# The opening of an attention stage: four first rotations on VectorE, the first row maxima in two parts, three loads of constants, and a new order of issue

## Chip, cores and metric

The kernel runs on one core of one Trainium2 chip. The metric is the device time of one execution in microseconds; the kernel before takes 635.73 us, the median of three runs between 634.97 and 636.86.

## What is computed

Three stages follow each other in one launch. Attention has 2 batches of 8 heads, 576 positions, 64 values per head, all in float32. A dense two-layer block (512 to 2048 to 512, leaky ReLU) takes its output, and a mixture of eight experts with the best two for each token takes that. The change touches attention alone:

```python
def rotate(x):
    x1, x2 = (x[..., :half], x[..., half:])
    return np.concatenate([x1 * cos - x2 * sin, x1 * sin + x2 * cos], axis=-1)
q_rot, k_rot = (rotate(q), rotate(k))
scores = scale * np.matmul(q_rot, k_rot.transpose(0, 1, 3, 2))
scores = scores - np.max(scores, axis=-1, keepdims=True)
attn = np.exp(scores)
attn = attn / (np.sum(attn, axis=-1, keepdims=True) + 1e-09)
return np.matmul(attn, v).astype(np.float32)
```

## The kernel before

Attention works through eight pairs of heads (pr = 0 to 7). The 576 positions of a head lie as five tiles j = 0 to 4 of 128 positions (the last one holds 64). A pair goes through these steps, each of which has a letter in the string ORDER (line 491):

- l (k for the first pair): the DMAs of q and k into raw; w: those of v. Part 0 of a load has the first 512 positions, part 1 the last 64. All go through SP's queue, apart from the first pair's second head and the constants, which go through ScalarE's queue.
- O on VectorE or P on GpSimd (POOL): the rotation ("rope"), four instructions: one product with cos (L299), two with sin, one for each half (L302), and one sum (L304). All of their inputs lie in SBUF. For the first pair each head is rotated for itself, so there are four ropes of four instructions on half-size tiles: q and k of head 0, q and k of head 1. FIRST_V (line 229) lists those on VectorE, FIRST_G those on POOL. All ropes of later pairs run on POOL.
- Q and K: TensorE transposes the rotated q and k into PSUM (L322, L324, L329). h and i: ScalarE copies them out as a rounded "high" part (L339). j and n: VectorE takes the rest as the "low" part (L343).
- M: for the row maxima, TensorE multiplies the high parts of q and k (L356), one tile of queries at a time. D: VectorE takes the maximum over the keys (L363 for the first pair, L368 later). J joins two halves of it (L374).
- R: TensorE turns the maxima into rows (L380); m: ScalarE copies those into MR (L384).
- S: the scores, keys on the partitions, as three products of high and low parts and one that takes MR off (L401). A cell is one tile j of keys by one half z (288) of the queries, both heads. W: ScalarE's exponential (L405).
- V: TensorE's product with v (L418). + on VectorE and ^ on POOL add exponentials (L425); G adds those up over the keys on TensorE (L434). U, t, T, s, B, N, X and Y divide by the sums and split the result into high and low for the dense block.
- The signs ! # $ % & * convert the dense block's first weights, o is a product on zeros that only keeps TensorE at work, c loads constants, f fills tiles on POOL, F and Z load weights and small inputs.

The order is written out by hand: every engine issues its instructions in the sequence in which their letters stand in ORDER, and each waits for its inputs and for the buffers it writes. The digit behind Q, K, M, R and S is one of three PSUM slots (two banks each) that the step writes; the step waits until the slot's last reader is done. A fourth pair of banks holds the products on zeros and later the output of V. The rotated tiles and their temporaries (rope_t) have two buffers each, which go round over (pair, q) and (pair, k). SP's queue follows ORDER as well.

After the last V of pair 7 TensorE goes on with the dense block (L570, L579), whose first part needs only the first batch's output.

Of the kernel before, what the change touches and what calls it, by code (L numbers as in the profile page):

```python
# [10 lines left out]
F32 = mybir.dt.float32  # L11
# [4 lines left out]
AF = mybir.ActivationFunctionType  # L16
# [5 lines left out]
B, H, S, D = 2, 8, 576, 64  # L22
# [3 lines left out]
KT = 5  # L26
# [10 lines left out]
_CUT = {}  # L37
# [44 lines left out]
def fused_kernel(ctx, tc, q, k, v, w_in, w_out, w_gate, w_noise, noise, w1, w2, consts, out):  # L82
    nc = tc.nc
    V, A, G, T = nc.vector, nc.scalar, nc.gpsimd, nc.tensor

    def pool(name, bufs=1, **kw):
        return tc.tile_pool(name=name, bufs=bufs, reuse_waits="tile", **kw)
# [23 lines left out]
    ident = const("ident")
# [109 lines left out]
    ct_att = ap.tile([128, NATT], F32, name="ct_att")  # L221
    a2 = att.enter_context(pool("att2", bufs=2))
    ps_s = att.enter_context(pool("ps_s", space=PSUM))
    ps_o = att.enter_context(pool("ps_o", space=PSUM))

    NP = B * 4
    NSET, NPB = 3, 10
    GROUPS, ADDERS = ((0, 1), (2, 3), (4,)), ((0,), (1,))
    FIRST_V, FIRST_G, ROPE_V = (('q', 0), ('k', 0), ('q', 1)), (('k', 1),), ()
    ET = mybir.EngineType  # L230
    order = ExitStack()
    order.enter_context(tc.manual_schedule(engines={ET.PE, ET.Activation, ET.DVE, ET.Pool}))
# [4 lines left out]
    raw, VF, VT, peak, MR = [], [], [], [], []  # L237
# [68 lines left out]
    def ps(n, name, shape=(128, 2, 512), dt=F32):  # L306
        return ps_s.tile(list(shape), dt, name=name, tag=f"s{n}")

    turned = {}

    def here(a):
        return slice(0, 128) if a is None else slice(64 * a, 64 * a + 64)

    def turn(pr, n, a, at):


        r = roped[pr, n][0]
# [12 lines left out]
        turned[pr, n, a] = p[:, :, :KT * 64].rearrange("p w (j n) -> p j w n", n=64)  # L330
# [39 lines left out]
    rows = {}  # L370
# [2 lines left out]
        with nc.allow_low_precision(reason="what is taken off is the same in a row's every place"):  # L373
            V.tensor_tensor(peak[pr % 2][:, :, 0:65:64].rearrange("p j h -> p h j"), halves[pr, 0], halves[pr, 1], op=OP.min)  # L374

    def max_turn(pr, at):
        p = ps(at, "pR")
        for j in range(KT):
            for w in range(2):
                T.matmul(p[:65, w, j * 64:(j + 1) * 64], peak[pr % 2][here(w), j], ident_r[here(w), here(w)], start=True, stop=True)  # L380
        rows[pr] = p[:65, :, :KT * 64].rearrange("p w (j n) -> p j w n", n=64)

    def max_rows(pr):
        A.activation(MR[pr % 2][:65].rearrange("p (j w n) -> p j w n", j=KT, w=2), rows[pr], AF.Copy)  # L384
# [104 lines left out]


    ORDER = (
"ckfcokkokkofokkokfoooooIOofoOoOoOoOQ0lOOoFohOoOZK1OlOooiOoloPM2wM0DPQ1lPDlM2hoPlDM0oPlDK2wjM0iwooPDlM1oPlDM0ol"
"DPM1oDM0oDPM1loDZQ0lnhPR1oomjoPoS2PS1WS0WS2PlWK1lWS0+liPVwVWnFPM2!S0DM1PWVDM2S0DM1PlWDS2lM0S1WDPWM2PQ0DM1hPDM2"
"VVDVj^lM1K2lDM0iVZ^DVlVJnwPM1R0wDS2mF+WS1PM0M2WDVP!GDPM1S0DGWPM2Q1DM0hGDS2PUjM0PWDtS1PM2WS0DlM1WS2wDPS0lW+S1ZW"
"K2PWS0Ti+M1sVPWwVDVwPVJnM0R1DBM2^mVDM0S1DPM2WVDM0S1DPM2WGDPM0S1DPS2W#Q0WS1hM2NVDWVjM2K1^DM0iVDVPGJnwM2S0lDPM1l"
"WGDlPM2US0DlS1PWl+M2VZWVwVDPlR0$lS1mM2lVPWtVDV^M0wS1DS2WP+S0WM1V^WVDM2S0DPS1WQ2WM0GPDhGTVjVPG%wM1PUK0sS2wDiPVt"
"VWnS1!PM2S0WBDVWJM1lS2DlR0W+Vlm^M1S2DS0W#S1NWM2V&DVW+PQ0M2S1hT^DsVWGwjlPM2S1DlM0PWGDFVM2S1PDS0WS2X+M1PVWGDWVYM"
"0wUS2DS1wJW+K0BWV*Vi^tVXnR2M1wPmVDV#M0M2S1DNVWDS0PXM1M2DGWVDPM1S0DS2W$Q1^WS0!M2VDhVPWVjYM2S0DS1W$S2PWM0GWPGDM1"
"US2DS0TWK1J%WVFVi^VwnR2wS0%msS1+WFM2VWD^V&M0S1DS2W+S0BWM1#V*WGwDV!tM2$S0M1WVDVGNDGVTsYM0US2DS1%&S0tWV+WVF+V&wV"
"#Xw*VwWS2$BS1WS0W^S2!M1VDWV^W%VM0M1M2VDN&GDGGYDXVJTR0#UsY$mtS1S2WBS0*WS1%WS2TWV+sV&*FVWZ+S0S1*WNS2BWS0WS1F^WGZ"  # L500
"VXV^WVVVNGGVYVXUYt")
    pairs = [(pr, n) for pr in range(NP) for n in "qk"]
    some = range(1, NP)
    both = [(0, n, a) for n in "qk" for a in range(2)]
    first = [(0, n, i, slice(a, a + 1), x) for a, x in enumerate((nc.sync, nc.scalar)) for n in "qk" for i in range(2)]
    spare = ps_o.tile([128, 2, 512], F32, name="pW", tag="o")
    cells = [(pr, j, z) for pr in range(NP) for j in range(KT) for z in range(2)]
    work = {"o": (lambda: busy(spare[:, 0]), [()] * ORDER.count("o")),
            "c": (lambda i: nc.scalar.dma_start(*((ct_att, consts[:, :NATT]), (ct, consts[:, NATT:NID]))[i]),
                  [(0,), (1,)]),  # L510
            "k": (load_qk, first),
            "l": (load_qk, [(pr, n, i, s) for pr, n in pairs[2:] for i, s in
                            [(0, slice(0, 2))] + ([(1, slice(0, 2))] if n == "q" else [(1, slice(a, a + 1)) for a in range(2)])]),
# [4 lines left out]
            "P": (rope, [(0, n, G, i, a, a + 1) for n, a in FIRST_G for i in range(4)] +  # L518
                  [(pr, n, G, i) for pr, n in pairs[2:] if (pr, n) not in ROPE_V for i in range(4)]),
            "Q": (turn, [(0, "q", 0), (0, "q", 1)] + [(pr, "q", None) for pr in some]),  # L520
            "K": (turn, [(0, "k", 0), (0, "k", 1)] + [(pr, "k", None) for pr in some]),
            "w": (load_v, [(pr, i) for pr in range(NP) for i in range(3)]),
            "M": (max_scores, [(0, a, j) for a in range(2) for j in range(KT)] +
                  [(pr, z, j) for pr in some for j in range(KT) for z in range(2)]),
            "S": (scores, cells), "W": (exp, cells), "V": (values, cells),
            "Z": (load_small, [(i,) for i in range(7)]), "F": (load_part, [(p,) for p in range(2 * NEARLY + 3)])}
# [543 lines left out]
    busy = nc.values_load(most, min_val=0, max_val=NT)  # L1070
    with tc.If(busy > C):
        with ExitStack() as rest:
# [13 lines left out]
            with tc.For_i(0, E, 1) as e:  # L1086
                n = nc.values_load(nparts[:, bass.ds(e, 1)], min_val=0, max_val=8)
                with tc.If(n > 0):
# [7 lines left out]
                    with tc.For_i(0, n, 1):  # L1096
# [4 lines left out]
                        t = bank[4][:CO, :5]  # L1101
# [49 lines left out]
```

## Time and profile before

| | us |
|---|---|
| runs: median, lowest, highest | 635.73, 634.97, 636.86 |
| the profiled execution's own time | 637.35 |
| its span, first to last instruction | 635.4 |
| TensorE's first score product (L401) | 19.66 |
| TensorE's first weights of the dense block (L570) | 149.03 |

TensorE counts as busy for 97% of the span, VectorE for 63%, ScalarE for 48%, POOL for 31%. In what follows PE is TensorE's products, PEld its weight loads, DVE is VectorE, ACT ScalarE, SP the queue that issues most DMAs. A row of the timeline gives the start and the duration in us, the engine, the line, what is written from what, how many instructions were merged into the row, and in brackets how long the engine was idle before it and what ended that. Products are pipelined, so the weight loads tell best when TensorE takes up a step.

### The profile page before, as it was taken

The page shows a single profiled execution, that of the slowest core. Times are in us where ns is not written, and L with a number is a line of the kernel's source. Part 1 is how long each engine was busy: PE and PEld are TensorE (multiplying, and loading weights), DVE is VectorE, ACT ScalarE, POOL GpSimd, SP SyncE. Part 2 cuts the span into 40 slices and gives each one's busy share as a digit, 9 for nine tenths or more (in the row PEclk, how much of TensorE's full clock was granted, in tenths as well). Part 3 has the DMA queues.
Part 4 walks back from the last instruction along what each step waited for, and adds up shares of the span by engine and source line. Part 5 has one row for each costly group of instructions (what it writes and reads, how often), then busy time and mean ns, then how long its engine had stood idle before and what let it go on. Part 6 is the DMA issues. An engine that isn't in the chain of part 4 may idle for free. (4 is left out here: it accounts for less than half of the span.)

```text
span 635.4 us, 12547 instructions
## 1 busy us (share of the span) xinstructions
PE 619.5 (97%) x4839; PEld 512.0 (81%) x4840; DVE 403.4 (63%) x844; ACT 303.3 (48%) x612; POOL 197.3 (31%) x203
## 2 busy tenths in 40 slices
PE   9999999999999999999999999999999999999993
PEld 4676676767888888897999768888888888888892
DVE  6788788784998888532476555647474747474511
ACT  2564565665554455222355414536453645454521
POOL 7999988354200000000000012140414141413202
PEclk9999999999999999999999999999999999999997
DMA  6332130333467544402744234485847585757413
GB/s 189 113 88 78 42 109 22 108 102 95 143 201 258 195 133 144 173 2 72 243 121 145 85 92 143 132 195 154 208 141 200 148 208 143 214 137 210 103 24 43
DMA packets 79167, 85.04 MB, mean 134 GB/s; under 512 B 11136, under 2 KB 60416, under 8 KB 79104
## 3 DMA queue, kind: packets, MB, share of 16 engines
q1 hardware_dynamic: 73760, 73.03, 38.1%
q0 software_dynamic: 4608, 10.49, 8.2%
q8 instruction: 39, 0.64, 0.4%
q10 hardware_dynamic: 736, 0.69, 0.4%
q14 instruction: 24, 0.20, 0.1%
HBM read 69.95 MB, written 14.19 MB: 132 GB/s over the span
## 5 line engine op out<-in xcount | busy, mean ns | idle before, releaser
L213 DVE TENSOR_TENSOR wl<-raw,wh 128x512 fp32r<-128x512 f32 x128 | 86.0, 687 | 63.0 <-ACT wh L211 55.3
L211 ACT ACTIVATE wh<-raw 128x512 fp32r<-128x512 f32 x128 | 78.8, 630 | 45.3 <-DMA raw<-in_moe_w 43.0
L1006 POOL DMA_INDIRECT out<-y_row,idx x24 | 41.9, 1744 | 175.0 <-ACT y_row L993 170.1
L982 PE MATMUL bank<-wh,g_x 128*128 128x512 f32 x256 | 93.2, 406 | 0.9 <-ACT g_x L964 0.7
L570 PE MATMUL bank<-xe_h,wl 128*128 128x320 f32 x256 | 79.4, 310 | 0.0
L570 PE MATMUL bank<-xe_h,wh 128*128 128x320 f32 x256 | 79.2, 309 | 0.0
L570 PE MATMUL bank<-xe_l,wh 128*128 128x320 f32 x256 | 78.7, 309 | 0.0
L591 ACT ACTIVATE g_t<-bank 128x512 f32<-128x512 f32 (+2 forms) x48 | 23.6, 491 | 91.4 <-PE bank L570 91.0
L873 POOL DMA_INDIRECT got<-x_rows,idx x24 | 25.2, 1050 | 133.1 <-DVE load L823 117.9
L579 PE MATMUL bank<-g_h,wh 128*128 128x512 f32 (+2 forms) x192 | 65.4, 341 | 0.0
L570 PE MATMUL bank<-xh,wh 128*128 128x512 f32 (+2 forms) x192 | 65.0, 338 | 0.0
L579 PE MATMUL bank<-g_l,wh 128*128 128x512 f32 (+2 forms) x192 | 64.7, 337 | 0.2 <-DVE g_l L599 0.2
L570 PE MATMUL bank<-xh,wl 128*128 128x512 f32 (+2 forms) x192 | 64.9, 338 | 0.0
L570 PE MATMUL bank<-xl,wh 128*128 128x512 f32 (+2 forms) x192 | 64.7, 337 | 0.0
L579 PE MATMUL bank<-g_h,wl 128*128 128x512 f32 (+2 forms) x192 | 64.5, 336 | 0.0
L405 ACT ACTIVATE p<-pS 128x576 f32<-128x576 f32 x80 | 49.2, 652 | 27.7 <-PE pS L401 27.4
L368 DVE TENSOR_REDUCE half<-pM 128x2 f32<-128x640 f32 x70 | 51.4, 753 | 16.4 <-PE pM L356 15.5
L592 DVE TENSOR_TENSOR g_f<-bank,g_t 128x512 f32<-128x512 f32 (+2 forms) x48 | 26.7, 556 | 50.6 <-ACT g_t L591 50.2
L982 PEld LDWEIGHTS bank<-wh,g_x 128*128 128x128 f32 x256 | 47.5, 188 | 12.3 <-DVE g_x L965 1.8
L570 PEld LDWEIGHTS bank<-xe_h,wh 128*128 128x128 f32 x256 | 48.2, 188 | 5.8 <-ACT xe_h L884 0.2
L570 PEld LDWEIGHTS bank<-xe_h,wl 128*128 128x128 f32 x256 | 48.1, 188 | 2.8
L982 PE MATMUL bank<-wl,g_x 128*128 128x512 f32 x128 | 50.0, 391 | 0.0
(192 smaller groups left out, 1354.9 us busy)
## 6 DMA issues: line engine op xcount, KB each, us to landing
raw<-in_moe_w SPq DMA_DIRECT2D x128, 256.0 KB
raw<-in_moe_w_in SPq DMA_DIRECT2D x16, 512.0 KB
raw<-in_moe_w_out SPq DMA_DIRECT2D x16, 512.0 KB
inv_sum<-inv_sums SPq DMA_DIRECT2D x16, 144.0 KB
out<-none SPq DMA_DIRECT2D x9, 256.0 KB
VF<-in_v SPq DMA_DIRECT2D x8, 256.0 KB
kept<-wh SPq DMA_DIRECT2D x4, 512.0 KB
kept<-wl SPq DMA_DIRECT2D x4, 512.0 KB
```

The lines of the kernel that those rows point to most:

```text
L211: A.activation(hi[:, part], t, AF.Copy)
L213: V.tensor_tensor(lo[:, part], t, f32(hi)[:, part], op=OP.subtract)
L368: V.tensor_reduce(halves[pr, i][:, :, j], p[:, :, :(320, 256)[i]], axis=AX.X, op=OP.max, negate=True)
L405: A.activation(t, scored.pop((pr, j, z))[:, :, 0:288], AF.Exp, scale=0.125)
L570: T.matmul(h[:, :n], w[:, 0, k * 128:(k + 1) * 128], m[:, k, cols:cols + n], start=(i == 0), stop=(i == 11))
L579: T.matmul(b[:, o:o + n], w[:, 1, ds], m[:, :n], start=(first and opens and t == 0), stop=(last and t == 2), skip_group_check=True)
L591: A.activation(t[:, :n], h[:, :n], AF.Copy, scale=0.01)
L592: V.tensor_tensor(g[:, :n], h[:, :n], t[:, :n], op=OP.max)
L873: G.indirect_dma_start(out=t[:n], out_offset=None, in_=x1_rows, in_offset=bass.IndirectOffsetOnAxis(ap=idx[e][:n, st:st + 1], axis=0))
L982: T.matmul(yr[st], s, w, start=(f == 0 and t == 0), stop=(f == 7 and t == 2))
L1006: s = G.indirect_dma_start(out=out, out_offset=bass.IndirectOffsetOnAxis(ap=idx[e][:n, st:st + 1], axis=0), in_=r[:n], in_offset=None, com ...
```

## The change

- FIRST_V takes all four ropes of the first pair; FIRST_G is empty. POOL's first rope is then that of pair 1.
- The constants come in three loads (cos, sin, ident) on ScalarE's queue instead of two (cos with sin, ident).
- The transposed k of the first pair's second head goes into the fourth pair of banks, not into a slot, and from then on the products on zeros write the unused end of that tile, 384 columns instead of 512.
- The first pair's row maxima come in two parts: tiles 0 to 2 of both heads, then tiles 3 and 4. R and m exist twice for that pair.
- The first pair's cells are sorted by half of the queries first: all five key tiles for z = 0, then those for z = 1. The first half needs the maxima of tiles 0 to 2 alone.
- ORDER is another string. All letters but O, P, R, m, c and o occur as often as before; o stands 33 times instead of 35. In the new string all sixteen O stand before the first D; the loads of pair 1 stand right behind those of the first pair, and the first weight load F, which stood between them, comes later.

```diff
-    FIRST_V, FIRST_G, ROPE_V = (('q', 0), ('k', 0), ('q', 1)), (('k', 1),), ()
+    FIRST_V, FIRST_G, ROPE_V = (('q', 0), ('k', 0), ('q', 1), ('k', 1)), (), ()
...
-    def turn(pr, n, a, at):
+    def turn(pr, n, a, at=None):
...
-            p = turned[pr, n, a] = ps(at, "pT", (128, 1024))
+            if at is None:
+                p = aside.append(ps_o.tile([128, 1024], F32, name="pT", tag="o")) or aside[0]
+            else:
+                p = ps(at, "pT", (128, 1024))
+            turned[pr, n, a] = p
...
+    def tiles(part):
+        return slice(0, KT) if part is None else (slice(0, 3), slice(3, KT))[part]
+
-    def max_turn(pr, at):
+    def max_turn(pr, part, at):
         p = ps(at, "pR")
-        for j in range(KT):
+        for j in range(KT)[tiles(part)]:
...
-    def max_rows(pr):
-        A.activation(MR[pr % 2][:65].rearrange("p (j w n) -> p j w n", j=KT, w=2), rows[pr], AF.Copy)
+    def max_rows(pr, part):
+        js = tiles(part)
+        A.activation(MR[pr % 2][:65].rearrange("p (j w n) -> p j w n", j=KT, w=2)[:, js], rows[pr][:, js], AF.Copy)
...
-"ckfcokkokkofokkokfoooooIOofoOoOoOoOQ0lOOoFohOoOZK1OlOooiOoloPM2wM0DPQ1lPDlM2hoPlDM0oPlDK2wjM0iwooPDlM1oPlDM0ol"
-"DPM1oDM0oDPM1loDZQ0lnhPR1oomjoPoS2PS1WS0WS2PlWK1lWS0+liPVwVWnFPM2!S0DM1PWVDM2S0DM1PlWDS2lM0S1WDPWM2PQ0DM1hPDM2"
...
+"ckfcokcokkofokkokfokoooOoIoOfoOooOOQ0OlOoohOloOK1lOOoloiOoOlQ2OOlM0hOM1PlDKwjM0ilooPDwM2oPlDM1oFDPM1oloDoooDPl"
+"Q2nwR1hM0oFoPmjowS1PDw!M2owDPWS0lM1WS2DPS0lW+K1lWM2lViPDVF!M0nPS2DWM1PVDM2R0DM1mPlM0DS2ZDlWM1PDM0S2PDM1WVPDM0S"
...
+    def load_table(i):
+        a, z = _CUT[("cos", "sin", "ident")[i]]
+        nc.scalar.dma_start(ct_att[:, a:z] if i < 2 else ct, consts[:, a:z])
+
...
+    def idle():
+        t = aside[0][:, 640:1024] if aside else spare[:, 0]
+        T.matmul(t, warm[:, :128], warm[:, :t.shape[-1]], start=True, stop=True)
+
-    cells = [(pr, j, z) for pr in range(NP) for j in range(KT) for z in range(2)]
+    cells = [(0, j, z) for z in range(2) for j in range(KT)]
+    cells += [(pr, j, z) for pr in some for j in range(KT) for z in range(2)]
...
-            "M": (max_scores, [(0, a, j) for a in range(2) for j in range(KT)] +
+            "M": (max_scores, [(0, a, j) for js in ((0, 1, 2), (3, 4)) for a in range(2) for j in js] +
...
+        work[n] = (f, [(0, 0), (0, 1)] + [(pr, None) for pr in some])
```

## Rows read from the trace of the kernel before

**Rows 1.** The page: TensorE's granted clock in 40 slices of the span.
```profile
PEclk9999999999999999999999999999999999999997
```

**Rows 2.** Waits of the weight loads, 148 to 300 us: us, times, longest.
```profile
PEld bank L703 <- issue: 2.9, 9, 0.3
PEld bank L579 <- DVE g_l L599: 0.7, 1, 0.7
```

**Rows 3.** Timeline of the weight loads: one late stretch of attention, and its end.
```profile
128.01 0.19 PEld L401 LDWEIGHTS pS<-high_q,high_k 64*128 64x128 f32 x2 [0.47 <-issue]
...
128.52 0.19 PEld L401 LDWEIGHTS pS<-high_q,high_k 64*128 64x128 f32 x2
...
130.48 1.13 PEld L418 LDWEIGHTS pO<-p,VF 128*32 128x32 f32 x24 [0.18 <-issue]
132.07 0.42 PEld L356 LDWEIGHTS pM<-high_k,high_q 64*128 64x128 f32 x6 [0.47 <-ACT p L405]
...
149.03 0.19 PEld L570 LDWEIGHTS bank<-xh,wh 128*128 128x128 f32 x1 [0.47 <-issue]
```

**Rows 4.** Timeline of VectorE in the opening.
```profile
4.71 0.49 DVE L299 TENSOR_TENSOR rope_q<-raw_q,ct_att 128x320 f32<-128x320 f32 x1 [3.44 <-DMA raw_q<-in_q]
...
8.50 0.49 DVE L304 TENSOR_TENSOR rope_q<-rope_q,rope_t 128x320 f32<-128x320 f32 x1
9.82 2.91 DVE L363 TENSOR_REDUCE peak<-pM 128x1 fp32r<-128x576 f32 x4 [0.82 <-PE pM L356]
...
14.35 3.88 DVE L363 TENSOR_REDUCE peak<-pM 128x1 fp32r<-128x576 f32 x5 [0.22 <-PE pM L356]
```

**Rows 5.** Timeline of POOL in the opening.
```profile
6.28 0.35 POOL L256 MEMSET VT<- 64x64 f32 x2
9.24 0.87 POOL L299 TENSOR_TENSOR rope_k<-raw_k,ct_att 128x320 f32<-128x320 f32 x1 [2.61 <-DMA raw_k<-in_k]
...
11.97 1.55 POOL L299 TENSOR_TENSOR rope_q<-raw_q,ct_att 128x640 f32<-128x640 f32 x1
13.47 1.68 POOL L302 TENSOR_TENSOR rope_t<-raw_q,ct_att 128x320 f32<-128x320 f32 x2
...
19.99 1.58 POOL L304 TENSOR_TENSOR rope_k<-rope_k,rope_t 128x640 f32<-128x640 f32 x1
```

**Rows 6.** Timeline of TensorE and ScalarE around the first scores.
```profile
17.68 0.52 PE L329 MATMUL pT<-ct,rope_q 64*128 64x64 f32 x10
18.25 0.70 ACT L339 ACTIVATE high_q<-pT 128x640 fp32r<-128x640 f32 x1 [4.67 <-PE pT L329]
...
18.87 0.70 ACT L384 ACTIVATE MR<-pR 65x640 fp32r<-65x640 f32 x1
19.66 0.40 PE L401 MATMUL pS<-high_q,high_k 64*128 64x288 f32 x2
...
21.88 0.48 PE L329 MATMUL pT<-ct,rope_k 64*128 64x64 f32 x10
```

**Rows 7.** Timeline of SP's queue: two DMA issues in the opening.
```profile
3.68 0.40 SPq L268 DMA_DIRECT2D raw_q<-in_q  x1
4.60 0.37 SPq L168 DMA_DIRECT2D raw<-in_moe_w_in  x1
```

**Rows 8.** Timeline of POOL from 102 us.
```profile
102.41 1.58 POOL L299 TENSOR_TENSOR rope_k<-raw_k,ct_att 128x640 f32<-128x640 f32 x1
103.94 1.62 POOL L425 TENSOR_TENSOR both<-p 128x576 f32<-128x576 f32 x1
105.52 1.30 POOL L302 TENSOR_TENSOR rope_t<-raw_k,ct_att 128x320 f32<-128x320 f32 x1
```

**Rows 9.** Timeline of VectorE beside it, and the same line alone.
```profile
102.97 1.31 DVE L200 TENSOR_SCALAR word<-word 128x512 int32<-128x512 int32 x1
104.31 1.80 DVE L201 SCALAR_TENSOR_TENSOR word<-raw,word 128x512 int32<-128x512 int32 x1
...
120.15 0.69 DVE L201 SCALAR_TENSOR_TENSOR word<-raw,word 128x512 int32<-128x512 int32 x1
```

**Rows 10.** Timeline of the weight loads: start and end of an early stretch.
```profile
25.73 0.19 PEld L356 LDWEIGHTS pM<-high_k,high_q 64*128 64x128 f32 x2 [0.47 <-DVE half L368]
...
30.10 1.13 PEld L418 LDWEIGHTS pO<-p,VF 128*32 128x32 f32 x24
```

More of the change, by code (lines that the diff above doesn't have):

```diff
@@ L491, in fused_kernel @@
     ORDER = (
-"ckfcokkokkofokkokfoooooIOofoOoOoOoOQ0lOOoFohOoOZK1OlOooiOoloPM2wM0DPQ1lPDlM2hoPlDM0oPlDK2wjM0iwooPDlM1oPlDM0ol"
-"DPM1oDM0oDPM1loDZQ0lnhPR1oomjoPoS2PS1WS0WS2PlWK1lWS0+liPVwVWnFPM2!S0DM1PWVDM2S0DM1PlWDS2lM0S1WDPWM2PQ0DM1hPDM2"
[L494 to L501, printed above, removed]
+"ckfcokcokkofokkokfokoooOoIoOfoOooOOQ0OlOoohOloOK1lOOoloiOoOlQ2OOlM0hOM1PlDKwjM0ilooPDwM2oPlDM1oFDPM0oloDoooDPl"
+"Q2nwR1hM0oFoPmjowS1PDw!M2owDPWS0lM1WS2DPS0lW+K1lWM2lViPDVF!M0nPS2DWM1PVDM2R0DM1mPlM0DS2ZDlM1WPDM0S2PDM1WVPDM0S"
+"2DS1W^l+K0WlQ2M1hVPDVijVG^nM1S2DM0WPVJDR1PM2#mGGDPM0S1DM2WPDS0Q1$WS2hPVWVjPM0wUS2DM1wPWDS0lM2lWS1DPZK0W+tS2M1W"
+"V+wVi^VlDVlnM2PS1DM0WVPDS2PJM1M0WDVVD^M2R1DM0mVDPM2S1DS0WTQ2PWsM1GDPhGPVjM0S1DM2PWDS0K1WM2GPDiVPnS0US2PM1WtVDW"
+"V#lM0S1JDlS2W+S0lWS1+lWM2^wVDWlG!lM0R1PDM2lmVTlDS0PwS1$WsS2PWM0wVWBD^S1%S2WM0BVWPVDlM1S2DZS0PW+K1M2iVGNWnGVDVP"
+"Q0UPM1S2DhPtVJVWjM1&wS2^DwS0W+ZR1WVPlmM2wS0DS1WTS2P%WM0VWPVDM1S2PDM0WVDM1NS2DM0WVD^Q1*K2hM0VXDGPiGjVXVnPM0wS1P"
+"DM2FWGPDsS0UJF+M1S2wWVYZWVDtR0M2^M1mDVV!BDM0S2DlS1W+S0lW^M2VD&VWM1YS2DS0W#M1GWPDVM2S0DPS1W#Q2WPM0VDhGPVjM1S0DN"
+"S2WTS1J+sWK0wWS2*i^VGWnwS1UB$S2M0!VwW%VZVWDtVX+VFM1M2R0DNwVmDZV&M1^S0DS2WTS1$sWYM0GXVWDS2S1+WS0BW+M2VW*GGDV#S1"
+"%UM0S2DWtVNWV!M1M0M2^D&VVDXV^DVVTJ$VsYGFS1wS0*wWR2wW%GBVm#V$&GS1U*S0%S2WtWVWS1NS0WS2&YS1WTV+sWVFVW*V^+S0S2WBS1"
+"W^GXFVVWYVGGVVNUXtY")
+    def load_table(i):
+        a, z = _CUT[("cos", "sin", "ident")[i]]
+        nc.scalar.dma_start(ct_att[:, a:z] if i < 2 else ct, consts[:, a:z])
     pairs = [(pr, n) for pr in range(NP) for n in "qk"]
@@ L506, in fused_kernel @@
     spare = ps_o.tile([128, 2, 512], F32, name="pW", tag="o")
-    cells = [(pr, j, z) for pr in range(NP) for j in range(KT) for z in range(2)]
-    work = {"o": (lambda: busy(spare[:, 0]), [()] * ORDER.count("o")),
-            "c": (lambda i: nc.scalar.dma_start(*((ct_att, consts[:, :NATT]), (ct, consts[:, NATT:NID]))[i]),
-                  [(0,), (1,)]),
+    aside = []
+    def idle():
[3 more added lines that the diff above has]
+    cells += [(pr, j, z) for pr in some for j in range(KT) for z in range(2)]
+    work = {"o": (idle, [()] * ORDER.count("o")),
+            "c": (load_table, [(0,), (1,), (2,)]),
             "k": (load_qk, first),
@@ L530, in fused_kernel @@
         work[m] = (turn_low, [(pr, x) for pr in range(NP)])
-    for n, f in (("R", max_turn), ("m", max_rows), ("U", take), ("t", sums), ("T", invert), ("s", sums_out), ("B", sums_in),
+    for n, f in (("R", max_turn), ("m", max_rows)):
+        work[n] = (f, [(0, 0), (0, 1)] + [(pr, None) for pr in some])
+    for n, f in (("U", take), ("t", sums), ("T", invert), ("s", sums_out), ("B", sums_in),
                  ("N", normalize), ("X", x_high), ("Y", x_low)):
```

## Prediction

> **What bounds the kernel now.** I read the page first: TensorE's granted clock is full in every slice but the last [rows 1], so no time is to be had or lost there. Then the waits of the weight loads behind attention: from 148 to 300 us one wait on data stands there, 0.7 us, the rest being gaps at a step of its own [rows 2]. The dense block thus starts when attention's last V is through, at 149.03 [rows 3], and what attention gains or loses the end of the kernel gains or loses. So the question is when TensorE finishes attention.
>
> Next, what TensorE does between its first score product at 19.66 [rows 6] and 149.03 [rows 3]: 129.4 us. Its steps cost what the late stretch shows, where nothing holds it up: a cell S takes 0.53 (four of them and one M from 128.01 to 130.48), three V take 1.59 from 130.48 to 132.07, 0.53 each, the gap of 0.47 before the next M being the last V still streaming, not a loss; going over to V leaves a gap of 0.18 [rows 3]. An M of a later pair is 0.13, what is left of that stretch. The Q and K of a pair are 0.48 each [rows 6]; G is about a V. By the letters of ORDER from the first S on: 80 S and 80 V are 84.8, 24 G 12.7, 70 M 9.1, 13 transposes 6.2, seven R about 2.5, and 39 changes to V or G and back at some 0.27 are 10.5. The sum is 126: of 129.4 us TensorE waits some 3.5. These are early: from 25.73 to 30.10 [rows 10] it does six M, three S and one transpose, 2.9 us of work in 4.4. Attention after the first S is therefore bound by TensorE's own work, and a change of its opening is worth the shift of the first S, less the work that it moves behind it, and what becomes of those 3.5 us.
>
> **The first S if nothing interferes.** Before, VectorE's three ropes run from 4.71 to 8.99, 1.4 each, and the first reduction starts at 9.82 [rows 4]. A fourth rope, whose letters stand before the first D, puts the end at 10.35: the first D comes 0.5 later. The data of head 1's k is no hindrance: POOL had it at 9.24 [rows 5] with 512 KB of w_in issued at 4.60 [rows 7] between, which now go later. From there six D (before: four in 2.91 and five in 3.88, 0.73 to 0.78 each [rows 4]) and one low part are 5.2; the sixth M writes the slot of the fifth, so one turnaround of some 0.7 comes in: 16.3. At about that time the five products on zeros, then Q of pair 1, are through. From a Q to ScalarE's copy are 0.57, that copy is 0.70, and MR's copy (0.70 before, three fifths as long now) follows [rows 6]: the first S comes at 18.1 instead of 19.66, a gain of 1.6, not the four reductions that the two parts seem to save.
>
> **What moves behind it.** Three M of the first pair (two products in one half of the array, one after the other, 0.27), the second R, a product on zeros: 1.2. The new string goes over to V or G 41 times instead of 39: two times 0.27 are 0.5. Together 1.7, so that this side is worth 0.1 us of loss with the waits as before. The Trainium skill, TensorEngine Tiling (Array Packing), section Tiling Modes, says that a change of tiling mode drains the engine; here a change from 64-row to 128-row products shows 0.18 us [rows 3], and if each were a full drain of 0.47 on the way back too, the two would cost 1.3 instead of 0.5.
>
> **The other edits.** The cos load alone is half as long, but VectorE's start was ended by raw_q [rows 4], which keeps its place in SP's queue: nothing, and a further issue on ScalarE's queue delays head 1's k by less than the time it has until 8.99. If that cover is gone, the delay goes into the fourth rope one for one. The transposed k in the fourth pair of banks frees a slot for an M: nothing to gain while VectorE is the pace. The second m is ScalarE's, which idles 4.67 before its copy for pair 1 [rows 6]. Products on zeros that are a quarter shorter, and two fewer: nothing, as long as the clock stays.
>
> **What the fourth rope meets on VectorE.** Before, POOL read no SBUF beside VectorE's ropes: it filled tiles until 6.63, then waited for head 1's k until 9.24, just after VectorE's 8.99, and began pair 1's q at 11.97 [rows 4, 5]. Now nothing stands on POOL before pair 1, and pair 1's q goes out at 3.68 as before, its second part at about 4.60, where w_in stood [rows 7]. POOL starts it at the earliest at 6.63, when its fills end, and at the latest near 9.24, when a load landed that had w_in ahead of it [rows 5]; I take 7.5 to 8, an estimate between these nearer to the lower end, since 512 KB are out of the way. VectorE is then in its third rope. And the two don't run side by side. At 102.97 VectorE starts a step on word while POOL is in a rope until 103.95: it takes 1.31. POOL's next add starts as the rope ends and ends at 105.56, held up a little; VectorE's next step, with two inputs in SBUF, starts at 104.31 and takes 1.80, ending at 106.11, against 0.69 alone; POOL's next one takes 1.30 [rows 8, 9]. Each engine goes on when the other's instruction ends: in turns.
>
> Priced so: POOL's first product (1.55 [rows 5]) comes between two instructions of VectorE's third rope: +1.5, ending at 10.4. POOL's next step writes the temporary of the first pair's q (two buffers go round), so it starts as that rope ends, beside the fourth rope. This has four instructions; between them come POOL's two half products (0.85 each, half of 1.68 [rows 5]) and its sum (1.55): in strict turns +3.0 us with small gaps. The fourth rope ends at 14.85 and not at 10.35, 4.5 late. The bound from the other side: rows 9 show turns where VectorE's next step needed the one before. A rope's three products need not wait for each other, and no row shows whether VectorE then keeps POOL out until the sum; if it does, only 1.5 and one half product come in between, about +2.3. The Trainium skill, SBUF — State Buffer, section Who interferes with whom, says that a VectorE instruction with two SBUF inputs and a GpSimd instruction that reads SBUF share one read interface, that the one to start first has it for its whole instruction, and that the other blocks fully. By that rule the strict reading holds, +4.5. Rows 8 and 9 agree with it; for independent instructions no row here tells. I take the middle, 3.4 us, for the row in hand is of the one kind and half of the rope's steps of the other.
>
> All that hangs on the first D (six D, the row maxima, the first S) moves with it: first S at 18.1 + 3.4 = 21.5. The D themselves read PSUM, and the row D beside POOL's rope from 9.82 shows no stretch [rows 4, 5].
>
> **Sum.** 21.5 + 129.4 + 1.7 = 152.6 instead of 149.03: +3.6 us. The profiled execution took 637.35, 1.6 above the median of the three runs and 0.5 above the slowest; on that it makes 640.95, and the same difference on the median of 635.73 makes 639.3.
>
> **Rivals.** (1) *The turns don't happen or cost nothing*: pair 1's q lands after 10.35, or VectorE's ropes go through first. Then the first S is at 18.1 and the sum is 0.1 to 0.2: 635.9, between 634 and 637.5. Against it: nothing goes ahead of that load now. For it: no row shows two ropes side by side. (2) *Faster, by the waits*: POOL's start of pair 1 at 7.5 to 8 instead of 11.97 brings its k from 21.57 (19.99 + 1.58 [rows 5], TensorE's K following at 21.88 [rows 6]) to about 17. If the early 3.5 us of waiting, which stand in the stretch behind that K [rows 10], come from POOL's pace, they go. With the first S at 18.1, the end is 18.1 + 129.4 + 1.7 - 3.5 = 145.7, -3.4: 632.3. It decides from the point where VectorE's fourth rope ends before about 12: later than that, the first S eats the gain. Against it: in 25.73 to 30.10 TensorE waited on VectorE's D [rows 10], and VectorE has a rope more to do. (3) *Slower still*: strict turns (+4.5), and the first pair's cells, which stood in a row before and now alternate with M and D over three slots, wait for reductions: a D is 0.73 to 0.78 against 0.53 of an S [rows 3, 4], some 0.22 for each of ten cells, 2.2. With 1.7 - 1.6 that is +6.8: 642.5.
>
> **How the numbers follow.** The forecast with (3) as its upper part 0.53, rival (1) 0.25, rival (2) 0.22. The predicted time is that of the forecast, 639.3; its own range is 637.7 to 642.5. The range for 8 in 10 goes from rival (2) to the top of (3): 632.3 to 642.5. Changes under 0.3%, 1.9 us, are about what a measurement of this kernel can't tell from none: faster by more 0.22, within 0.25, slower by more 0.53.
>
> **What would show it.** In the new profile, VectorE's O of the third and fourth rope with durations of 1 to 2 us in place of 0.3 to 0.49, POOL's L299 of pair 1 before 9, the first D between 12.5 and 15, the first S between 20 and 22.5, TensorE's first dense weights at 151 to 156, and from some 60 us on no waits of TensorE. The prediction is wrong if the O keep their durations (then rival 1 or 2, told apart by the excess of TensorE's stretches before 50 us), or if the first dense weights come later or earlier than the first S says: then the new order's waits behind it decide, which I have only bounded.

## The result, and the profile after

The changed kernel takes 644.04 us (median of five runs, 643.25 to 644.91) against 635.73 of the kernel before, a ratio of 1.0125 with a 95% interval of 1.0107 to 1.0142. That is 8.3 us slower. The forecast was 639.3, slower by 3.6, with 642.5 as the upper end of the range: the sign held, the size is more than double, and the time lies outside the range.

Two corrections to the text ahead. In the new string as quoted there two places are miscopied: its first line ends in ...DM1oFDPM0oloDoooDPl, and its second has DlM1WPD where DlWM1PD is shown. So the sixth M of the first pair writes slot 0, not the slot of the fifth, and the step of the prediction that adds a turnaround of 0.7 us rests on a letter that isn't there.

In the kernel after, the lines have moved: M is L360, the first pair's D L367, later ones L372, J L378, low parts L347, R L387, S L409, V L426, the adds L433, the products on zeros L523, the dense block L590.

First the page's row of the granted clock:

```profile
PEclk9799999999999999999999999999999999999997
```

Then a table of stretches (columns: stretch, its length, busy time and count on PE, PEld, DVE, ACT and POOL, granted clock, DMA share, GB/s):

```profile
4.00:12.00 8.00, 6.97 (x34) 3.69 (x32) 7.11 (x15) 2.00 (x3) 5.05 (x13) 1.00 0.55 158
12.00:13.00 1.00, 0.08 (x1) 0.00 (x0) 0.97 (x2) 0.10 (x1) 0.92 (x2) 1.00 0.70 139
13.00:14.00 1.00, 0.00 (x0) 0.00 (x0) 1.00 (x1) 0.00 (x0) 1.00 (x1) 0.78 0.57 194
14.00:22.00 8.00, 7.33 (x22) 3.91 (x22) 5.61 (x8) 0.70 (x1) 7.92 (x8) 0.50 0.84 262
22.00:24.00 2.00, 2.00 (x21) 1.42 (x20) 0.86 (x2) 0.78 (x2) 1.92 (x3) 0.55 0.72 192
24.00:30.00 6.00, 6.00 (x71) 4.21 (x70) 5.32 (x7) 4.65 (x8) 5.77 (x5) 1.00 0.49 149
```

The second slice is a 7 where [rows 1] has a 9. In the table, TensorE does next to nothing from 12 to 14 us, the clock falls in the second half of that, and for ten microseconds it runs at 0.50, 1.2 GHz instead of 2.4. Nothing in the forecast has this.

VectorE's timeline, the lines that answer to [rows 4]:

```profile
4.35 0.49 DVE L299 TENSOR_TENSOR rope_q<-raw_q,ct_att 128x320 f32<-128x320 f32 x1 [3.08 <-POOL VT L256]
...
8.12 1.89 DVE L302 TENSOR_TENSOR rope_t<-raw_q,ct_att 128x160 f32<-128x160 f32 x2
10.05 0.49 DVE L304 TENSOR_TENSOR rope_q<-rope_q,rope_t 128x320 f32<-128x320 f32 x1
...
10.86 1.88 DVE L302 TENSOR_TENSOR rope_t<-raw_k,ct_att 128x160 f32<-128x160 f32 x2
12.77 1.74 DVE L304 TENSOR_TENSOR rope_k<-rope_k,rope_t 128x320 f32<-128x320 f32 x1
14.44 0.74 DVE L367 TENSOR_REDUCE peak<-pM 128x1 fp32r<-128x576 f32 x1
...
18.36 0.76 DVE L367 TENSOR_REDUCE peak<-pM 128x1 fp32r<-128x576 f32 x1 [0.83 <-PE pM L360]
```

POOL's, which answer to [rows 5]:

```profile
8.21 1.62 POOL L299 TENSOR_TENSOR rope_q<-raw_q,ct_att 128x640 f32<-128x640 f32 x1 [0.86 <-DMA raw_q<-in_q]
10.62 1.94 POOL L302 TENSOR_TENSOR rope_t<-raw_q,ct_att 128x320 f32<-128x320 f32 x2 [0.79 <-DVE rope_q L304]
12.63 1.53 POOL L304 TENSOR_TENSOR rope_q<-rope_q,rope_t 128x640 f32<-128x640 f32 x1
```

And TensorE's, which answer to [rows 6], with the first weights of the dense block from the timeline of the weight loads, which answer to [rows 3]:

```profile
14.66 1.30 PE L328 MATMUL pT<-ct,rope_k 128*128 128x128 f32 x5 [2.58 <-DVE rope_k L304]
15.89 0.85 PE L360 MATMUL pM<-high_k,high_q 64*128 64x320 f32 x2
...
24.54 0.40 PE L409 MATMUL pS<-high_q,high_k 64*128 64x288 f32 x2
...
157.51 0.19 PEld L590 LDWEIGHTS bank<-xh,wh 128*128 128x128 f32 x1 [0.47 <-issue]
```

POOL begins pair 1's q at 8.21, and from then on VectorE's ropes stretch: two half products take 1.89 and 1.88 instead of 0.55, the sum 1.74 instead of 0.49, 1.34 + 1.33 + 1.25 = 3.9 us in all. The fourth rope is TensorE's next input, so TensorE idles for 2.58 us, and what it does then runs at half clock: a pair of M takes 0.85, against 0.53 in e1_hold below, and a D waits up to 0.83 for it. The first S comes at 24.54 instead of 19.66, the dense block at 157.51 instead of 149.03.

### The profile page after: what moved, and what is told of

Same layout as the page of the kernel before. It is cut to its first block, busy times and chain, and to the rows that moved or that the text cites. A ratio compares the mean times of both kernels' runs of the same rounds, so it can differ in the third digit from the quotient of the medians.

```text
span 642.3 us, 12554 instructions
## 1 busy us (share of the span) xinstructions
PE 622.0 (97%) x4837; PEld 514.1 (80%) x4838; DVE 412.5 (64%) x848; ACT 302.7 (47%) x613; POOL 193.0 (30%) x199
## 5 line engine op out<-in xcount | busy, mean ns | idle before, releaser
L590 PE MATMUL bank<-xe_h,wl 128*128 128x320 f32 x256 | 79.4, 310 | 0.0
L590 PE MATMUL bank<-xe_h,wh 128*128 128x320 f32 x256 | 79.2, 309 | 0.0
L590 PE MATMUL bank<-xe_l,wh 128*128 128x320 f32 x256 | 78.7, 309 | 0.0
L590 PE MATMUL bank<-xh,wh 128*128 128x512 f32 (+2 forms) x192 | 65.0, 338 | 0.0
L590 PE MATMUL bank<-xh,wl 128*128 128x512 f32 (+2 forms) x192 | 64.9, 338 | 0.0
L590 PE MATMUL bank<-xl,wh 128*128 128x512 f32 (+2 forms) x192 | 64.7, 337 | 0.0
L372 DVE TENSOR_REDUCE half<-pM 128x2 f32<-128x640 f32 x70 | 51.4, 754 | 16.4 <-PE pM L360 15.8
L590 PEld LDWEIGHTS bank<-xe_h,wh 128*128 128x128 f32 x256 | 48.2, 188 | 5.9 <-ACT xe_h L904 0.2
L590 PEld LDWEIGHTS bank<-xe_h,wl 128*128 128x128 f32 x256 | 48.1, 188 | 2.8
```

Source lines behind the costliest of these rows:

```text
L372: V.tensor_reduce(halves[pr, i][:, :, j], p[:, :, :(320, 256)[i]], axis=AX.X, op=OP.max, negate=True)
L590: T.matmul(h[:, :n], w[:, 0, k * 128:(k + 1) * 128], m[:, k, cols:cols + n], start=(i == 0), stop=(i == 11))
```

## The experiments

Three theories stood against each other. The first: the turns of VectorE and POOL in the opening make the loss. The second: the granted clock, which falls in the pause that the turns make, is a part of its own. The third: the new order makes TensorE wait behind the first S; what spoke for it is an add of POOL (the letter ^) that idled 6.21 us for an exponential at 38.39 us, with POOL's ropes queued behind it. Ratios below are to the kernel before on the same chip, whose medians were 636.27 (e1 to e4), 636.68 (e5 to e8) and 636.62 (e9 to e11). There are four runs each of e2 and e3, six of e7, seven of e9 and ten of the others.

| kernel | median, us | ratio, 95% interval | first S | dense block |
|---|---|---|---|---|
| before | 635.73 | | 19.66 | 149.03 |
| after | 644.04 | 1.0125 (1.0107 to 1.0142) | 24.54 | 157.51 |
| e1_hold | 634.96 | 0.9980 (0.9964 to 0.9996) | 17.49 | 149.00 |
| e2_warm | 641.03 | 1.0077 (1.0048 to 1.0105) | 22.18 | 154.66 |
| e3_adds | 644.25 | 1.0128 (1.0098 to 1.0157) | 24.47 | 156.62 |
| e4_hold_adds | 637.29 | 1.0010 (0.9986 to 1.0034) | 17.76 | 152.06 |
| e5_k1_pool | 636.88 | 1.0014 (0.9982 to 1.0047) | 17.92 | 149.60 |
| e6_old_four | 644.89 | 1.0113 (1.0077 to 1.0148) | 26.97 | 158.66 |
| e7_w_in_first | 643.62 | 1.0108 (1.0074 to 1.0142) | 24.07 | 156.56 |
| e8_fill_pool | 635.66 | 0.9979 (0.9959 to 0.9999) | 17.75 | 149.00 |
| e9_old_four_warm | 639.93 | 1.0063 (1.0034 to 1.0093) | 21.86 | 152.02 |
| e10_old_four_hold | 637.74 | 1.0023 (1.0004 to 1.0042) | 21.16 | 151.07 |
| e11_hold_two_loads | 635.40 | 0.9980 (0.9961 to 0.9999) | 17.43 | 149.18 |

Behind the first dense weights, which no edit touches, the thirteen traces take between 483.5 and 486.4 us to their end. One trace therefore doesn't tell a difference of 1 or 2 us between two medians.

**e1_hold: the kernel after, with POOL's first rope made to wait for VectorE's fourth.**

```diff
-...OOlM0hOM1PlDKwjM0i...
+...OOlM0hO@M1PlDKwjM0i...
+    scr = ap.tile([128, 1], F32, name="scr")
+    work["@"] = (lambda: G.tensor_copy(scr, roped[0, "k"][0][:, 4, 1, 63:64]), [()])
```

> The changed kernel, but POOL begins pair 1's rope only when VectorE's fourth rope is done: one copy of a single column that reads the fourth rope's result stands ahead of POOL's first P. Theory 1 (VectorE's ropes and POOL's rope take turns at SBUF, and that is most of the loss): the half products and the sum of ropes three and four go back to 0.3 and 0.49 us, the fourth rope ends at 10.3 to 10.8 instead of 14.4, TensorE is not left without work for over 2 us, so its clock stays full, and the first S comes at 18 to 19 instead of 24.5; time 637 to 639. Rival (the loss lies in the new order behind the first S): the first S moves, but the end by less than 2 us: 642 or more.

POOL's and VectorE's timelines, TensorE's first S and the first dense weights:

```profile
10.71 0.18 POOL L561 COPY scr<-rope_k 128x1 f32<-128x1 f32 x1 [2.90 <-DVE rope_k L304]
10.94 1.54 POOL L299 TENSOR_TENSOR rope_q<-raw_q,ct_att 128x640 f32<-128x640 f32 x1
...
9.48 0.56 DVE L302 TENSOR_TENSOR rope_t<-raw_k,ct_att 128x160 f32<-128x160 f32 x2
10.06 0.49 DVE L304 TENSOR_TENSOR rope_k<-rope_k,rope_t 128x320 f32<-128x320 f32 x1
10.84 0.76 DVE L367 TENSOR_REDUCE peak<-pM 128x1 fp32r<-128x576 f32 x1 [0.28 <-PE pM L360]
12.24 3.42 DVE L367 TENSOR_REDUCE peak<-pM 128x1 fp32r<-128x576 f32 x5
...
17.49 0.40 PE L409 MATMUL pS<-high_q,high_k 64*128 64x288 f32 x2
...
149.00 0.19 PEld L592 LDWEIGHTS bank<-xh,wh 128*128 128x128 f32 x1 [0.47 <-issue]
```

POOL starts 2.7 us later than in the kernel after, and all 8.3 us are gone: VectorE's products take 0.56 for two again, the first D comes at 10.84, the granted clock is 1.00 in all of the opening. Everything else of the change is still there, so the loss comes from POOL's early rope and what follows from it. It also shows what the change is worth without the turns: the first S is 2.17 us earlier than before, and the dense block starts within 0.03 us of where it did. From the first S to the dense block it takes 131.51 us instead of 129.37. Its median is 1.3 us below that of the kernel before all the same; where that comes from, the two traces don't show.

**e2_warm: the kernel after, with 14 more products on zeros while TensorE waits for the fourth rope.**

```diff
-...OOlM0hOM1PlDK...
+...OOlM0hOM1ooooooooooooooPlDK...
```

> The changed kernel with 14 more products on zeros between the second M and the transposes that wait for the fourth rope, so that TensorE is at work while VectorE and POOL take turns. Theory 2 (a part of the loss is the clock, which fell to half from 13.6 to 23.9 us after TensorE stood idle): the first D stays at 14.4, the clock stays full, the six D and what follows take 8 us instead of 10.1, the first S comes at 22 to 22.7; time 641.5 to 642.5. Rival (what follows the first D is VectorE's pace whatever the clock): first S within 0.5 us of 24.5, time 643.5 to 644.5.

Stretches, with columns as above:

```profile
10.00:11.00 1.00, 0.00 (x0) 0.00 (x0) 0.96 (x4) 0.00 (x0) 0.00 (x0) 1.00 0.00 0
...
12.00:14.00 2.00, 2.00 (x12) 1.00 (x11) 1.97 (x3) 0.51 (x1) 1.92 (x3) 1.00 0.73 229
14.00:22.00 8.00, 7.53 (x50) 4.12 (x49) 6.95 (x10) 1.65 (x3) 7.92 (x8) 1.00 0.81 248
```

The fourth rope and the first D on VectorE's timeline:

```profile
11.27 1.88 DVE L302 TENSOR_TENSOR rope_t<-raw_k,ct_att 128x160 f32<-128x160 f32 x2
13.19 1.75 DVE L304 TENSOR_TENSOR rope_k<-rope_k,rope_t 128x320 f32<-128x320 f32 x1
14.86 0.74 DVE L367 TENSOR_REDUCE peak<-pM 128x1 fp32r<-128x576 f32 x1
```

The turns are as long and the first D comes even later, at 14.86, yet the clock stays full, the first S comes 2.4 us earlier than in the kernel after, and the time is lower. Against the kernel before of the same chip e2 is 4.8 us slower and e1 1.3 faster: the turns with their consequences cost 6.1. The kernel after is 8.3 slower than its own kernel before: some 3.5 are left for the clock. By its interval e2's 4.8 may be 3.1 to 6.7, so the split is good to some 2 us. By the start of the dense block the shares are 5.66 and 2.85.

**e3_adds and e4_hold_adds: the second ^ moved behind the exponential that it awaits, and two G moved with it; e3 is the kernel after, e4 is e1.**

```diff
-2DS1W^l+K0WlQ2M1hVPDVijVG^nM1S2DM0WPVJDR1PM2#mGGDPM0S1DM2WPDS0Q1$WS2hPVWVjPM0wUS2D...
+2DS1W^l+K0WlQ2M1hVPDVijVGnM1S2DM0WPVJDR1PM2#mDPM0S1DM2WPDS0Q1$WS2hPVWV^jPM0wGGUS2D...
```

> The changed kernel with the first pair's second add on POOL moved behind five more of POOL's rope steps, and the two G that need it moved to just before U. Theory 3 (the order behind the first S costs some 2.4 us because that add waits 6.2 us for an exponential with the rope of pair 3 queued behind it): POOL's idle time of 6.2 us at 32 to 38 goes, TensorE's stretch at 49 us loses its 2.4 us of excess; time 641 to 642. Rival (the ropes have time to spare, and TensorE waits there for VectorE): 643.5 to 644.5.

> Both: POOL held until the fourth rope is done, and the second add moved back. If the causes add up: 6 us and 2.4 us less, 635.5. If the earlier first S also shortens the add's wait (its exponential comes 6 us earlier), the move gains little here: 636.5 to 638.

POOL's idle time of 6.21 us is gone from the trace of e3, and its time is that of the kernel after. So the third theory falls in the form in which it was put: that wait cost nothing that the time shows. In e4 the same edit on top of e1 is 2.3 us worse than e1, and its dense block starts at 152.06. Stretches of e4, with columns as above:

```profile
30.00:40.00 10.00, 8.86 (x132) 6.23 (x129) 9.85 (x13) 4.49 (x7) 9.92 (x8) 0.98 0.11 31
40.00:50.00 10.00, 9.77 (x140) 7.07 (x142) 7.21 (x10) 5.86 (x9) 6.57 (x6) 0.85 0.25 66
```

The granted clock falls there too. How much of the 2.3 us is the order itself and how much the clock can't be told from this kernel, but not all is the clock: the five runs of e4 whose mean granted clock, 0.994 to 0.996, is that of e1's runs took 636.3 to 637.6, the ten of e1 633.8 to 636.8.

**e5_k1_pool: the kernel after with the fourth rope on POOL, as before.**

```diff
-    FIRST_V, FIRST_G, ROPE_V = (('q', 0), ('k', 0), ('q', 1), ('k', 1)), (), ()
+    FIRST_V, FIRST_G, ROPE_V = (('q', 0), ('k', 0), ('q', 1)), (('k', 1),), ()
-...loiOoOlQ2OOlM0hOM1PlDK...
+...loiOoPlQ2PPlM0hPM1PlDK...
```

> The changed kernel, new order and all, with the fourth rope (k of head 1) back on POOL: its four letters are P again. Theory 1 (turns between VectorE's ropes and POOL's rope of pair 1): POOL's rope of pair 1 now stands behind its rope of head 1's k, so only the third rope on VectorE meets POOL, in shorter steps (0.87 and 0.5 us); the first D comes at 10 to 11, the clock stays full, first S at 17.5 to 19; time 635 to 637. Rival (the new order or the three loads of constants carry the loss): 641 or more.

```profile
8.38 0.86 POOL L299 TENSOR_TENSOR rope_k<-raw_k,ct_att 128x320 f32<-128x320 f32 x1 [0.73 <-DMA raw_k<-in_k]
...
8.47 1.11 DVE L304 TENSOR_TENSOR rope_q<-rope_q,rope_t 128x320 f32<-128x320 f32 x1
```

These are POOL's and VectorE's timelines: one turn is left, 0.6 us on VectorE's last sum. The first S is at 17.92, 0.4 later than in e1, and the time equals that of before. So with three ropes on VectorE the new order costs nothing, and with four and turns it costs 8.3. Four ropes alone don't make the loss either, as e1 has them: it hangs on the fourth rope on VectorE together with POOL's early start.

**e6_old_four: the kernel before with that one edit, the fourth rope on VectorE.**

```diff
-...iOoloPM2wM0DPQ1lPDlM2hoPlDM0oPl...
+...iOoloOM2wM0DOQ1lODlM2hoOlDM0oPl...
```

> The kernel before with one part of the change alone: the fourth rope on VectorE, its letters where POOL's four stood (between the first D), old order of loads. Theory 1: POOL begins pair 1's q as soon as it has landed, 9.3 to 11, while the fourth rope runs from 8.9 on between the first D; one to three turns of 0.85 to 1.55 us stretch it, and the gain of POOL's earlier start is of the same size: 635 to 638, with some O of 1 us and more. If the fourth rope by itself cost what the whole change cost: 642 or more.

Stretches, with columns as above:

```profile
12.00:13.00 1.00, 0.00 (x0) 0.00 (x0) 1.00 (x2) 0.00 (x0) 1.00 (x2) 1.00 0.09 20
13.00:14.00 1.00, 0.59 (x2) 0.50 (x2) 1.00 (x3) 0.00 (x0) 0.92 (x2) 0.54 0.14 33
14.00:22.00 8.00, 7.67 (x22) 4.03 (x21) 4.85 (x7) 0.70 (x1) 7.92 (x7) 0.50 0.49 131
22.00:26.00 4.00, 4.00 (x28) 2.15 (x27) 2.55 (x4) 1.04 (x2) 3.92 (x4) 0.50 0.74 229
```

TensorE's and VectorE's timelines:

```profile
13.41 0.85 PE L356 MATMUL pM<-high_k,high_q 64*128 64x320 f32 x2 [1.44 <-DVE peak L363]
...
11.00 1.70 DVE L302 TENSOR_TENSOR rope_t<-raw_k,ct_att 128x160 f32<-128x160 f32 x2
```

One edit in the old order makes the whole loss, 8.2 us, where 635 to 638 was expected. POOL starts only at 10.07 here, so fewer turns fall on VectorE, but TensorE idles 1.44 us for it, and the clock stays at half until past 26 us. Nine of the ten runs took 643.2 to 648.3 us with a mean granted clock of 0.980 to 0.986, and one took 636.78 with 0.994. No trace was taken of that one. The next two kernels split this loss.

**e9_old_four_warm: e6 with seven more products on zeros ahead of the fourth rope's transposes. e10_old_four_hold: e6 with the wait of e1.**

```diff
-...DlM2hoOlDM0oPl...
+...DlM2hooooooooOlDM0oPl...    (e9)
+...DlM2hoO@lDM0oPl...          (e10, with the copy of e1)
```

> The kernel before with one edit of the change, the fourth rope on VectorE, and seven more products on zeros behind the first pair's second h, where TensorE stood idle in the fourth kernel of the turns (from 11.98 to 13.41 us in e6_old_four). Theory: of the 8.2 us that this edit costs in the old order the turns are the smaller part, and the clock that falls to half behind that pause is the larger one. Then here VectorE's L302 keep 1.7 to 1.9 us for two, the granted clock stays at 1.00 up to 40 us, the first S comes at 20 to 22, and the time is 637 to 640. Rival, the turns alone make the loss: the time stays at 643 to 646 although the clock is full.

> The kernel before with the fourth rope on VectorE, and POOL held back until that rope is done by a copy of one column of it. No new order, no parts of the row maxima, no third load. Theory: without turns the edit costs nothing, because VectorE is through with its fourth rope at 10.4 to 10.7 and TensorE's pause stays short: L302 of the fourth rope 0.5 to 0.6 for two, the granted clock 1.00 up to 40 us, the first S at 19 to 20.5, the time 634.5 to 637.5. Rival: in the old order the fourth rope is late for TensorE in any case (its transposes stand where POOL's rope was awaited), the clock falls, and the time is 642 to 646 as in e6_old_four.

VectorE's fourth rope in e9, then in e10:

```profile
11.10 1.41 DVE L302 TENSOR_TENSOR rope_t<-raw_k,ct_att 128x160 f32<-128x160 f32 x2
```

```profile
11.27 0.55 DVE L302 TENSOR_TENSOR rope_t<-raw_k,ct_att 128x160 f32<-128x160 f32 x2
```

In both the granted clock is 1.00 from 10 to 30 us. Against the kernel before of the same chip e10 is slower by 1.1, e9 by 3.3, e6 by 8.2. So in the old order the fourth rope's place on VectorE costs 1.1 by itself (with the wait), the turns 2.2, and the clock 4.9: a smaller delay than in the new order, but a dearer clock. By the intervals in the table e9's 3.3 may be 2.2 to 5.9. And the one run of e6 at full clock was no slower than the kernel before: if the turns happened in it too, the clock's part is larger still, but that run has no trace.

**e7_w_in_first: the kernel after with the 512 KB of w_in (the first F) again between the loads of pair 1.**

```diff
-...OQ0OlOoohOl...   ...DlM1oFDPM0o...
+...OQ0OlFOoohOl...  ...DlM1oDPM0o...
```

> The changed kernel with the first weight load back between pair 1's first load and the rest, as it was before, so that pair 1's q lands later. Theory 1: POOL's L299 of pair 1 starts at 9.5 to 11 instead of 8.2, after the third rope; at most the fourth rope is in turns, and the first D comes at 10.5 to 13; time 636 to 641, the later POOL starts the less. If the time of landing doesn't matter: 643.5 to 644.5.

```profile
10.11 1.64 POOL L299 TENSOR_TENSOR rope_q<-raw_q,ct_att 128x640 f32<-128x640 f32 x1 [2.47 <-DMA raw_k<-in_k]
...
10.27 2.56 DVE L302 TENSOR_TENSOR rope_t<-raw_k,ct_att 128x160 f32<-128x160 f32 x2
```

These are POOL's and VectorE's timelines. Pair 1's q starts 1.9 us later than in the kernel after and spares VectorE's third rope, but it meets the fourth one in full: two half products take 2.56. VectorE also waits 0.42 for the fourth rope's data. The first D is 0.6 us earlier, TensorE idles 3.04 us, the clock falls all the same, and the time can't be told from that of the kernel after. A shift of POOL by 1.9 us isn't enough; it must be off VectorE's back until the fourth rope is through.

**e8_fill_pool: the kernel after with five fills of 128x640 on POOL ahead of its first rope, in place of the wait.**

```diff
-...OOlM0hOM1PlDK...
+...OOlM0hO@M1PlDK...
+    scr = ap.tile([128, 640], F32, name="scr")
+    work["@"] = (lambda: [G.memset(scr, 0.0) for _ in range(5)], [()])
```

> The changed kernel with POOL kept busy instead of waiting: five fills of a scratch tile (0.64 us each, writes only) stand ahead of its first P, from 7.4 to about 10.5. If it is POOL's reading that takes turns with VectorE, ropes three and four keep 0.3 and 0.49 us a step beside the fills and the kernel is as fast as the one that waits: 634.5 to 636. If any work of POOL stretches VectorE's ropes: their steps take 0.9 to 1.1 us and the time is 638 or more.

```profile
7.77 3.39 POOL L561 MEMSET scr<- 128x640 f32 x5
...
9.53 0.55 DVE L302 TENSOR_TENSOR rope_t<-raw_k,ct_att 128x160 f32<-128x160 f32 x2
```

POOL is at work beside VectorE's third and fourth rope (its timeline and VectorE's), and VectorE's two half products take 0.55 as if alone. So it isn't any work of POOL that stretches VectorE's ropes, but work that reads SBUF. A fill differs from a product in more than that; but POOL's small cast of ident, which reads SBUF too, takes 0.62 in e8 where it falls on a rope of VectorE, at 5.38, and 0.29 in the kernel before. The Trainium skill, SBUF — State Buffer, section Who interferes with whom, says this: a VectorE instruction with two inputs in SBUF contends with a GpSimd instruction that reads SBUF, not with one that only writes it. The rows of e8 and of the kernel after agree with both halves.

**e11_hold_two_loads: e1 with the constants in two loads again.**

```diff
-"ckfcokcokkofok...
+"ckfcokokkofok...
```

(The load of cos takes sin with it again; the letter c stands twice.)

> e1_hold with the constants in two loads again, cos and sin together, as before the change. Theory: the third load is worth nothing or a few tenths at the start: VectorE's first product starts at 4.6 to 4.8 instead of 4.35, the first S comes 0.2 to 0.4 later than the 17.49 of e1_hold, and the time is within 1 us of it, 634 to 636.5. Rival: the split load is what the new opening rests on, and the time rises to 637.5 or more.

VectorE's first product starts at 4.82, in e1 at 4.86, the first S at 17.43, the time within 0.5 us of e1. (The kernel after starts it at 4.35 and e7 at 4.17, with the same three loads as e1: that start varies by itself.) The third load is worth nothing here. No version beats the kernel before by more than 0.2%: e1, e8 and e11 are 1.0 to 1.3 us faster, with intervals that end at 0.9996 and 0.9999.

## Why the prediction was right or wrong

**What held.** The bound: a shift of the first S reaches the dense block (from e1 to the kernel after, 7.05 there become 8.51), and the new order alone is worth nothing. The forecast had 0.1 us of loss for it, and e1 has the dense block at 149.00 against 149.03. Its two halves were both somewhat short: the lead of the first S is 2.17, forecast 1.6, and the work moved behind it 2.14, forecast 1.7. The lead is larger because the turnaround of 0.7 that came from the miscopied slot doesn't exist: in e1 the last five D take 3.42, one after the other. The mechanism also held: pair 1's data comes sooner, POOL's first rope meets VectorE's third and fourth, and they run in turns. POOL started at 8.21, forecast 7.5 to 8.

**What failed.** The forecast for the first dense weights was 152.6, measured 157.51: 4.91 short. Three steps make it up.

1. *The size of the turns: 0.69.* The first D was forecast at 13.75, the middle between the bounds; it came at 14.44. The turns cost 3.9 us instead of 3.4. The doubt behind the middle value was whether VectorE's products that don't depend on each other also let POOL in between. They do: two half products of one rope, 0.55 together, took 1.88. So the strict reading is the right one, every step of POOL came in between; but a turn costs somewhat less than POOL's step is long, 1.34 for a product of 1.62, and the sum lies between the middle value and the strict 4.5. In e2, too, the first D is 4.02 later than in e1.

2. *The clock: 2.35.* "No time is to be had or lost there" was the step that failed. It was read from a kernel in which TensorE had no such pause, and the forecast itself put a delay of 3.4 us into TensorE's input without asking what TensorE does meanwhile. From the first D to the first S the forecast had 7.75 us; e1 has 6.65 and e2 7.32 at full clock, the kernel after 10.10 at half clock. So the clock itself costs 2.78 in this stretch, of which 0.43 don't show in the miss, as the forecast had 7.75 where e2 has 7.32. The prediction even wrote that fewer products on zeros cost nothing "as long as the clock stays", and stopped there. The longer upper case, rival (3), was longer for a reason that didn't show: a chain of alternating cells and D, priced at 2.2, for which the 131.51 of e1 against 131.1 leave 0.4.

3. *Behind the first S: 1.87.* 132.97 us to the dense block instead of 131.1. The prediction had named a dense block later than the first S says as a sign of being wrong. Of the 1.87, 0.41 is the moved work (131.51 in e1). The rest I followed cell by cell through S in the kernel after and in e1: the kernel after is 7.05 late at the first cell, 6.72 at the tenth, 8.34 at the fifteenth, and then 8.30 to 8.39 until the last. So the remaining loss falls into one stretch, from 41.0 to 51.7 us of the kernel after. Its weight loads there, and VectorE:

```profile
43.23 0.40 PEld L387 LDWEIGHTS pR<-ident_r,peak 64*65 64x65 f32 x10 [1.31 <-issue]
51.12 0.19 PEld L360 LDWEIGHTS pM<-high_k,high_q 64*128 64x128 f32 x2 [1.46 <-DVE low_q L347]
...
41.96 1.15 DVE L378 TENSOR_TENSOR peak<-half,half 128x10 fp32r<-128x10 f32 x1
46.86 1.49 DVE L200 TENSOR_SCALAR word<-word 128x512 int32<-128x512 int32 x1
48.38 1.95 DVE L201 SCALAR_TENSOR_TENSOR word<-raw,word 128x512 int32<-128x512 int32 x1
```

The same two weight loads in e1, and J (L378) there:

```profile
35.68 0.37 PEld L387 LDWEIGHTS pR<-ident_r,peak 64*65 64x65 f32 x10 [0.47 <-issue]
42.78 0.19 PEld L360 LDWEIGHTS pM<-high_k,high_q 64*128 64x128 f32 x2 [0.75 <-DVE low_q L347]
...
35.34 0.16 DVE L378 TENSOR_TENSOR peak<-half,half 128x10 fp32r<-128x10 f32 x1
```

J joins ten columns; it takes 0.16 alone and 1.15 when a rope of POOL (a sum from 41.54 on, 1.54 long) is ahead of it, and R waits for it. The low part of q waits behind two conversions that take 1.49 and 1.95 beside POOL's ropes and 0.42 and 0.69 in e3. The two waits are 0.84 and 0.71 longer than in e1, together 1.55, about the 1.6 by which the shift grows there. So these are turns too, later ones. They aren't chance: e2 and e7, the other two kernels with early turns and with nothing changed behind the first S, have nearly the same pair of waits, 1.31 and 1.44, and the same J. In e2:

```profile
39.30 1.15 DVE L378 TENSOR_TENSOR peak<-half,half 128x10 fp32r<-128x10 f32 x1
```

In e5, e8 and e11, where POOL's rope comes later in the opening, J takes 0.16 to 0.54. This is read from rows; no kernel was made that takes these two away alone. e3 has them shorter and its dense block 0.9 us earlier, but its median is no better.

**The rivals.** (1), the turns don't happen, is what e1 shows when they are taken away, not what the change does. (2), the earlier k of pair 1 takes away TensorE's early waits, did not show: even in e1, from the first S on, nothing is gained. (3) has the sign and nearly the size of the top of the range, by the wrong steps.

## What to carry to other kernels

Before work is moved onto VectorE to get it off POOL, look at what POOL will do in the freed time: if it reads SBUF and VectorE's instructions have two inputs there, the two run in turns, even where each engine's own instructions don't depend on each other, and a ten-column step can wait a microsecond for one of its instructions. When a delay of some microseconds goes into the input of TensorE, ask in the same step what keeps TensorE busy meanwhile; a pause can cost more by the clock than it lasts: here some 3.5 us for 2.58, and 4.9 for 1.44. Both are cheap to test: hold the other engine back with a small copy, and fill the pause with products on zeros.

## What was not expected of the hardware

- A step of ten columns can cost a microsecond: J went from 0.16 to 1.15 us by a POOL instruction that had started before it. The first pair's reductions, which read PSUM, took 0.74 to 0.76 beside POOL's ropes in the kernel after.
- POOL's fills, 0.68 us each in e8 (3.39 for five), left VectorE's ropes at 0.49 and 0.55; POOL's products stretched them more than four times (2.56 instead of 0.55 in e7).
- The granted clock went to its lower level, 1.2 GHz, in pauses of TensorE of 2.58 us (kernel after) and 1.44 us (e6), and stayed there until about 24 and past 26 us though TensorE was busy again from 14.66 and 13.41. In e2 it stayed full through a pause of 1.33 us, and in e4 it fell at 39.5 us, until 42.9, though no pause from 30 us on was longer than 0.44: the length of one pause doesn't say by itself whether it falls. The price was about 3.5 us in the new order and 4.9 in the old one, more than the turns' own 2.2 there.
- The times of the kernel with the shorter pause, e6, fall into two groups, 636.78 and 643.2 to 648.3, and one run of e5 took 644.57 while nine took 635.5 to 637.7. The mean granted clock of the runs goes with the groups: 0.994 against 0.980 to 0.986 in e6, 0.983 against 0.993 to 0.996 in e5. So in these two kernels the clock falls in some executions and not in others; what decides it isn't shown.
